# Windowed attention and gated feed-forward on one core: first loads of q and k in two pieces, a new load order, zero products in planned gaps, new priorities

## The chip, the cores and the metric

The kernel runs on one core of a Trainium2 chip. A core has TensorE (PE, matrix products, with a weight-load path shown as PEld), VectorE (DVE), ScalarE (ACT), GpSimd (POOL) and SyncE (SP), and 16 DMA engines that all queues share. POOL and SP issue the DMAs here. The metric is device time in microseconds (us), median over runs; the kernel before takes 314.26 us in the median of three runs (313.21 to 316.16).

## The reference

Eight batches of 576 tokens, eight heads of 64. Causal attention over a window of 64 tokens, and then a feed-forward layer with a ReLU gate over all 4608 tokens:

```python
scores = scale * np.matmul(q, k.transpose(0, 1, 3, 2))
mask = (rel >= 0) & (rel < window)          # rel = query - key, window = 64
attn = softmax(np.where(mask, scores, -1e9))
x = (attn @ v).transpose(0, 2, 1, 3).reshape(4608, 512)
gate = np.maximum(x @ w_gate, 0.0)          # w_gate, w_val: 512 x 1536
val = x @ w_val
out = (gate * val) @ w_out                  # w_out: 1536 x 512
```

## The kernel before

**Tiling.** The 4608 tokens are nine tiles of 512 (`TT`), counted 0 to 8. Attention goes by windows of 64 queries, nine to a batch (`NG`), eight to a tile; so tile 0 is windows 0 to 7 of batch 0, and tile 1 the last window of batch 0 and windows 0 to 6 of batch 1, which are its rows 0 to 447. A window's scores are products of transposed k and q (line 354, after a bias product that brings the mask, line 346); ACT takes the exponential into `p` (607); products of p with v and a column of ones give values and sums (360); DVE takes the reciprocal (622), normalises into `xw` (367) and transposes into `xt` (372).

**Feed-forward.** Tile 0 goes directly: products with `wg` and `wv` (712), ReLU on ACT (721), product of the two on DVE (723), output products (877). Tiles 1 to 8 use Strassen-like forms with seven products in place of eight (803 for gate and value, 965 for output from tile `TF` = 3 on). They need sums of weights `us`, `vs` (752), sums of x (678), and later `ts` (910). Results come out of PSUM by ACT copies (812, 850) and DVE sums (819); POOL multiplies gate and value (837).

**Loads.** q and k of a batch come as four loads, two names by two halves of the heads `hh`, 576 rows each: `qk_load` (316) on POOL, cast to 16 bits on the way, one partition holding 18 rows of one head. DVE transposes each with one instruction, `qk_trans` (322). v comes by `v_load` (325), the weights by `w_part` (306) in blocks of four column groups, two loads a block, and `wo_part` (309) in three blocks. In the first part q and k of `hh` = 0 go by SP without a cast into the space of `vs` (381), and ACT and DVE cast them (404).

**Order.** Nothing is left to a scheduler at run time. `first_part` (from line 376) is written by hand: tile 0's first six windows, with zero products (`PADS`, `keep_hot`) among them. Everything else is made by `second_part` as operations of a `Plan`: each has a due key, the engines that can do it with a duration for each, what it comes after, and what it takes and gives of pools (PSUM banks, buffers). `Plan.run` simulates the engines and issues, whenever an engine is free, the ready operation of the smallest key; that order becomes each engine's instruction stream. The engine then takes its stream in order, so an instruction that waits holds up all behind it on its engine. The keys are sums of constants in the table `K` (line 21), such as `T1` and `STEP` for when tile 1 and each later tile is due.

**What the plan knows of queues.** Loads on one queue follow one another in the plan (`dma=(MB, rate, queue)`); POOL has at most eight DMAs in flight. PE's instructions come in blocks of 256, which the plan fetches (`fetch`, `ASK`, `NEED`), counting two for each product of an operation's `count`. The runs of small products, scores and values, are put off if the fetch would be late. Before, the direct products of tile 0 (712) have no count.

Of the kernel before, what the change touches and what calls it, by code (L numbers as in the profile page):

```python
# [19 lines left out]

K = {"T1": 43.37, "STEP": 31.65, "wo1": 25.425, "wo2": 25.425, "q0": 0.14, "q1": 3.42, "q10": 0.5, "q11": -2.79, "v": 2.23, "v1": 24.04, "ql": 0.01, "qt": -1.77, "qti": 4.63, "vl": 1.83, "vc": 1.99, "vm": 1.89, "e": 6.47, "gap": 2.43, "gap1": -2.13, "r": -0.09, "tn": 2.56, "xf": 5.88, "wf": -6.38, "wfj": -2.26, "sn": 0.0, "su": -1.66, "re": 17.19, "mu": -7.51, "la": -4.87, "o0": 29.92, "o0j": 1.82, "o0s": -3.73, "oo": -0.002, "os": 0.141, "oj": 4.12, "gs": -2.63, "fo": -0.031, "fi": 0.104, "fs": 1.88, "fu": 1.51, "W0": 85.11, "TF": 3, "rs": -3.06, "rv": -0.95, "rt": -2.24, "slack": 0.3, "d2": 8.63}

# [4 lines left out]
class Op:  # L27


    def __init__(self, name, key, engines, fn, after, take, give, dma):  # L30
        self.small = 0
        self.count = 0
        self.name = name
        self.key, self.engines, self.fn = key, engines, fn
        self.take, self.give, self.dma = take, give, dma
        self.left = len(after)
        self.feeds = []
        self.ready = dict.fromkeys(engines, 0.0)
        self.end = None
        self.on = None  # L40


class Plan:
# [5 lines left out]
    TURN = 0.093  # L49
    FLIGHT = 8  # L50
# [4 lines left out]
    def __init__(self, free, queue, pools):  # L55
# [3 lines left out]
        self.home = {id(x[2]): name for name, items in self.pools.items() for x in items}  # L59
        self.known = {e: [] for e in free}  # L60
# [48 lines left out]

    def finish(self, o, e, t, dur):  # L110
        if e == "PE":
            dur += self.TURN * ((o.small > 0) != self.small)
            self.small = o.small > 0
            if o.count:
                dur = self.fetch(2 * o.count, t, dur, True) - t
# [25 lines left out]
    def grab(self, o, e, t):  # L141
# [7 lines left out]
        for holder, names, items in got:  # L149
            for name, item in zip(names, items):  # L150
                self.pools[self.home[id(item[2])]].remove(item)
                holder[name] = item[2]
        return None

    def pick(self, e, t):
# [6 lines left out]
        for o in sorted(self.known[e], key=lambda o: (o.key - self.STAY * (e == "PE" and self.small and o.small), o.n)):  # L162
            if o.ready[e] > t + 1e-9:
                continue
            if e == "POOL" and o.dma and self.flight[0] + 0.1 > t + 1e-9:
                continue
# [19 lines left out]
    def run(self, emit):  # L186
# [7 lines left out]
        while left:  # L194
# [3 lines left out]
            t = heapq.heappop(self.times)  # L198
            moved = True
            while moved:  # L200
                moved = False
                for e in ("PE", "ACT", "DVE", "POOL", "SP"):
# [9 lines left out]
                    if port:  # L212
                        other = "POOL" if e == "DVE" else "DVE"
                        begin = max(t, self.port[other])
                        self.port[e] = begin + dur
                    self.finish(o, e, begin, dur)
# [8 lines left out]
def kernel(  # L225
# [16 lines left out]
    G = 4  # L242
# [68 lines left out]
    def heads_of(b, name, hh):  # L311
        src = (q if name == "q" else k)[b, G * hh:G * hh + G]
        return src.rearrange("h (i j) d -> (h i) (j d)", i=32)

    def qk_load(b, name, hh):
        nc.gpsimd.dma_start(nat[name, hh], heads_of(b, name, hh))

    def qk_trans(b, name, hh):
        src = nat[name, hh].bitcast(FP32).rearrange("p (j e) -> p j e", e=32)
        dst = qTs[b % 2][:, hh] if name == "q" else kTs[b % 2][:, hh, 64:64 + S]  # L320
# [53 lines left out]
    PADS = 72  # L374

    def first_part():

        n = S // 32 * D
        t32 = {name: vs.rearrange("p a k n -> p (a k n)").bitcast(FP32)[:, n * i:n * i + n] for i, name in enumerate("kq")}
        for name in "kq":  # L380
            nc.sync.dma_start(t32[name], heads_of(0, name, 0))
        for name in "kq":
            qk_load(0, name, 1)
# [40 lines left out]
        qk_trans(0, "k", 0)  # L424
        rounded("q", nc.scalar.copy, nc.vector.tensor_copy)
        qk_trans(0, "q", 0)
        for name in "kq":
            qk_trans(0, name, 1)
# [18 lines left out]
        for hh in range(2):  # L447
            copies(0, nc.vector.tensor_copy, G * hh, G * hh + G)
            values(0, hh)
        copies(1, nc.gpsimd.tensor_copy, 0, H)  # L450
# [28 lines left out]
    def second_part():  # L479

        plan = Plan({"PE": 14.3, "ACT": 16.2, "DVE": 16.8, "POOL": 13.2, "SP": 3.0},
                    {"q": 16.4, "sp": 3.0},
                    {"bank": list(zip((13.4, 13.4, 15.2, 15.9, 12.9, 12.9, 12.9), banks)), "bo": [(14.2, banks[7])],
                     "p": [(13.8 if i < 8 else 0.0, p) for i, p in enumerate(ps)],
                     "pr": [(0.0, x) for x in prs]})
        plan.at = 428 + 2 * PADS
        plan.asked, plan.got, plan.come = 2, 1, [13.0, 22.2]
# [22 lines left out]

        T0 = 16.0
# [8 lines left out]
        for n, (wt, src, key) in enumerate(((wg, moe_w_gate, "g"), (wv, moe_w_val, "v"))):  # L520
            for blk in range(NF // 4):
                loaded[key, blk] = [None, None] if blk == 0 else [
                    op("w_load", 14.0 + 4.0 * blk + 2.0 * n + 0.1 * a, issue(0.7),
                       lambda e, wt=wt, src=src, blk=blk, a=a: w_part(wt, src, 4 * blk, 4 * blk + 4, a),
                       dma=(0.524, 0.40, "q")) for a in range(2)]
        for blk in range(NF // 4):
            loaded["o", blk] = [op("wo_load", (24.5, K["wo1"], K["wo2"])[blk], issue(0.75), lambda e, blk=blk: wo_part(4 * blk, 4 * blk + 4),
# [10 lines left out]
        def quad_key(t, hh):  # L538
            return period(t - 1) + (K["q0"], K["q1"])[hh] if t > 1 else T0 + K["q10"] + K["q11"] * hh

        def values_key(t):
            return period(t - 1) + K["v"] if t > 1 else T0 + K["v1"]

        def load_batch(b):
            need = quad_key(max(1, NG * b // 8), 0)
            for i, (name, hh) in enumerate((n, hh) for hh in range(2) for n in "kq"):
                before = [turns[b - 1, name, hh]] if b > 1 else []
                key = 24.6 + 0.1 * i if b == 1 else need - K["ql"] + i
                loads[b, name, hh] = op("qk_load", key, issue(0.57), lambda e, b=b, name=name, hh=hh: qk_load(b, name, hh),
                                        after=before, dma=(0.59, 0.40, "q"))  # L550
                turns[b, name, hh] = op("qk_turn", need - K["qt"] + K["qti"] * i, {"DVE": (1.245, False)},
                                        lambda e, b=b, name=name, hh=hh: qk_trans(b, name, hh),
                                        after=[loads[b, name, hh]] + (score_ops[b - 2] if b > 1 else []))

        def load_values(b):
            parts = {0: ((1, 0, 128), (3, 0, 128)), 1: ((5, 0, 128),), 2: ((7, 0, 128), (NG - 1, 64, 128))}
            for uu in range(UB):
                need = values_key(max(0, (NG * b + 3 * uu - 8)) // 8 + 1)
                if (b, uu) not in ((0, 0), (0, 1)):
                    for n, part in enumerate(parts[uu]):  # L560
                        key = {(0, 2): 16.9, (1, 0): 25.4, (1, 1): 25.41, (1, 2): 25.42 + 0.1 * n}.get((b, uu), need - K["vl"])
# [13 lines left out]
                elif b == 1:  # L575
                    vcopies[b, uu] = [op("v_copy", need - K["vc"], {"ACT": (0.17 + 0.42 * to.shape[1], False), "DVE": (0.1 + 0.2 * to.shape[1], True),
# [3 lines left out]
                else:  # L580
                    before = value_ops[b - 2] if b > 1 else []
                    vcopies[b, uu] = [op("v_move", need - K["vm"], {"SP": (0.6, False)}, lambda e, to=to, at=at: nc.sync.dma_start(to, at),
# [9 lines left out]
        def attend(items, key):  # L592
# [5 lines left out]
            after = [turns[b, nm, hh] for b in batches if b for hh in halves for nm in "kq"]  # L598
# [6 lines left out]
            for g in range(G):  # L605
                def exp(e, g=g):
                    nc.scalar.activation(pp[g][:, 0:n].rearrange("p n c -> p (n c)"), st[g][:, 0:64 * n], ACT.Exp, scale=scale)  # L607
                exps.append(op("exp", key + K["e"] + 0.6 * g, act(64 * n), exp, after=[run], take=[("p", pp, (g,))], give=[("bank", st, g)]))
            return pp, exps

        def value_bank(t, key, parts, before, gives, last):
# [19 lines left out]
            r = op("recip", key + K["r"], {"DVE": (0.17, False)}, recip, after=[a])  # L631
            return a, op("norm", key + K["r"] + 0.3, dve(64 * m), normed, after=[r] + last, give=[("bank", to, "b")])
# [4 lines left out]
        def attend_tile(t):  # L637
# [9 lines left out]
            gap = K["gap"] if t > 1 else K["gap1"]  # L647
# [16 lines left out]
            for hh in range(2):  # L664
                for i in range(2):
                    lo = 16 * hh + 8 * i
                    turned[t].append(op("turn", key + K["tn"] + gap * (1.2 * (2 * hh + i) + 1.7), {"DVE": (0.712, False)},
# [6 lines left out]
            for n, (x, y) in enumerate(((b12, b11), (b22, xc[:, 0]), (b22, b12), (b21, xc[:, 1]))):  # L674
                after = [(t11, t12), (t22,), (t22, t12), (t21,)][n] + tuple(free)
                after += tuple(forms[j] for j in {1: (0,), 3: (1,)}.get(n, ()))
                forms.append(op("x_form", key + K["xf"] * gap + n, {**pool(512), **(dve16(512) if n == 1 or t == 1 else {})},
# [3 lines left out]

        load_values(0)
        pp, masks = attend([(6 + i, hh) for hh in range(2) for i in range(2)], T0 + K["rs"])
        rest, before = [], []
        for hh in range(2):
            parts = [(24 + 4 * hh + s, pp, 6 + s // 2, hh, 2 * hh + s // 2, s % 2) for s in range(4)]
            gives = [("p", pp, g) for g in range(G)] if hh else []
            a, o = value_bank(0, T0 + K["rv"] + 0.3 * hh, parts, masks + before, gives, [])
# [378 lines left out]
```

## Time and profile before

The page describes one execution, which took 313.09 us; its span from first to last instruction is 311.1 us.

| what | us |
|---|---|
| median of three runs | 314.26 |
| the profiled execution, its span | 313.09, 311.1 |
| PE busy | 297.9 |
| DVE, POOL, ACT busy | 244.5, 228.0, 214.4 |
| POOL's product of gate and value, 96 times | 121.1 |
| score and value products, 1152 each, busy | 13.0 and 15.4 |
| transposes of q and k, 32 times, each | 1.24 |
| DMA issue on POOL for q or k, each | 0.57 to 0.58 |

Matmuls are pipelined: one of 256 columns shows 273 ns from start to modelled end, but in a row they start 109 ns apart. So busy time of PE tells where it has nothing to do at all, and not how dense it is. PEclk is the granted clock of TensorE. DMA share is the mean busy share of the 16 DMA engines, and can go over 1 where packets overlap. "issue" is time in which an engine waited for nothing that the profile shows. An entry "[1.05 <-DVE qT L322]" is idle time before an instruction and what ended it.

### The profile page before, as it was taken

The numbers are of one execution on the slowest core, as the hardware profiler recorded it, in microseconds if no ns is written. First come the engines' busy times: TensorE is split into PE (matmuls) and PEld (weight loads), VectorE is DVE, ScalarE is ACT, GpSimd is POOL, SyncE is SP. The second block draws the span as 40 slices with busy tenths as digits, with TensorE's granted clock in tenths as the row PEclk, the third lists the DMA queues.
The fourth block names the chain that finished last, engine by engine and source line by source line (L and its number), as shares of the span: only waits on it lengthen the run. The fifth ranks groups of instructions, "written<-read, shape, count | busy, mean of one in ns | idle before, by whom it ended". The sixth has DMA issues, their size and how long they took to land.

```text
span 311.1 us, 11209 instructions
## 1 busy us (share of the span) xinstructions
PE 297.9 (96%) x4749; PEld 240.4 (77%) x4749; DVE 244.5 (79%) x421; ACT 214.4 (69%) x415; POOL 228.0 (73%) x232
## 2 busy tenths in 40 slices
PE   7699969999999999999999999999999999999994
PEld 4487734588867786778888888888888888888883
DVE  5969986799946985887897999899876896674951
ACT  4553363598788589668868786888588968678731
POOL 8689896488997998699499946992479258737530
PEclk9889989999999999999999999999999999999999
DMA  7999998999139955777698183912102010121034
GB/s 216 188 174 206 194 198 144 197 201 101 28 31 192 188 117 112 124 120 104 94 108 100 52 152 62 138 52 68 39 2 71 15 59 2 36 67 36 1 103 135
DMA packets 58930, 32.87 MB, mean 106 GB/s; under 512 B 39424, under 2 KB 53248, under 8 KB 58880
## 3 DMA queue, kind: packets, MB, share of 16 engines
q0 software_dynamic: 46672, 18.29, 49.9%
q1 hardware_dynamic: 12208, 13.87, 14.2%
q8 instruction: 37, 0.61, 0.8%
q14 instruction: 13, 0.11, 0.1%
HBM read 37.75 MB, written 9.44 MB: 152 GB/s over the span
## 4 chain that ended last, share of the span: by engine, by line
PE 80%; DMA 10%; POOL 4%; DVE 2%; issue 2%; ACT 0%; SPq 0%; POOLq 0%; DVEq 0%; ACTq 0%
PE bank L803 46%; PE bank L965 18%; PE bank L877 9%; PE bank L360 4%; DMA q<-in_q_dram 3%; DMA wv<-in_moe_w_val_dram 2%; PE bank L354 2%; DMA v<-in_v_dram 2%; DMA v<-v 2%; PE bank L346 1%; POOL v L325 1%; DVE xt L372 1%; DVE xw L367 1%; POOL v L578 0%; POOL wg L306 0%
## 5 line engine op out<-in xcount | busy, mean ns | idle before, releaser
L837 POOL TENSOR_TENSOR g_sb<-pr,pr 128x512 f16<-128x512 f32 x96 | 121.1, 1278 | 48.7 <-ACT pr L850 18.1
L819 DVE TENSOR_TENSOR pr<-bank,pr 128x512 f32<-128x512 f32 x144 | 93.4, 682 | 33.5 <-PE bank L803 29.8
L812 ACT COPY pr<-bank 128x512 f32<-128x512 f32 x144 | 80.7, 589 | 35.6 <-PE bank L803 30.4
L803 PE MATMUL bank<-xt,us 128*128 128x256 f16 x384 | 56.2, 273 | 0.1
L803 PE MATMUL bank<-xt,vs 128*128 128x256 f16 x384 | 56.2, 273 | 0.0
L828 ACT ACTIVATE pr<-pr 128x512 f32<-128x512 f32 x72 | 45.0, 635 | 8.4 <-DVE pr L819 8.1
L803 PE MATMUL bank<-xt,wv 128*128 128x256 f16 x288 | 42.4, 272 | 0.1
L803 PE MATMUL bank<-xt,wg 128*128 128x256 f16 x288 | 41.9, 273 | 0.0
L803 PEld LDWEIGHTS <-us 128*128 128x128 f16 x384 | 37.1, 98 | 6.1 <-issue 0.3
L803 PEld LDWEIGHTS <-vs 128*128 128x128 f16 x384 | 37.0, 98 | 6.1
L607 ACT ACTIVATE p<-bank 128x512 f16<-128x512 f32 (+1 forms) x68 | 35.7, 591 | 7.0 <-PE bank L354 6.9
L877 PE MATMUL bank<-wo,g_sb 128*128 128x512 f16 x144 | 36.8, 393 | 0.0
L325 POOL DMA_DIRECT2D v<-in_v_dram x40 | 34.8, 877 | 0.3 <-DMA wo<-in_moe_w_out_dram 0.3
L850 ACT ACTIVATE pr<-bank 128x512 f32<-128x512 f32 x48 | 27.4, 596 | 6.8 <-PE bank L803 6.2
L803 PEld LDWEIGHTS <-wv 128*128 128x128 f16 x288 | 28.2, 98 | 4.1 <-issue 0.3
L803 PEld LDWEIGHTS <-wg 128*128 128x128 f16 x288 | 27.8, 98 | 4.0
L965 PEld LDWEIGHTS <-g_sb 128*128 128x128 f16 x288 | 27.5, 98 | 3.5
L965 PE MATMUL bank<-wo,g_sb 128*128 128x256 f16 x216 | 28.7, 273 | 0.0
L367 DVE TENSOR_TENSOR xw<-bank,r 128x448 f16<-128x448 f32 (+2 forms) x45 | 25.9, 576 | 1.5
L372 DVE STREAM_TRANSPOSE xt<-xw 128x512 f16<-128x512 f16 (+2 forms) x38 | 25.1, 671 | 0.5 <-ACT xw L473 0.3
L877 PEld LDWEIGHTS <-g_sb 128*128 128x128 f16 x144 | 13.9, 101 | 13.3 <-issue 2.2
L965 PEld LDWEIGHTS <-ss 128*128 128x128 f16 x216 | 21.1, 98 | 2.4
(95 smaller groups left out, 386.2 us busy)
## 6 DMA issues: line engine op xcount, KB each, us to landing
out_dram<-pr SPq DMA_DIRECT2D x35, 256.0 KB, 2.8
k<-in_k_dram POOLq DMA_DIRECT2D x15, 288.0 KB, 6.6
q<-in_q_dram POOLq DMA_DIRECT2D x15, 288.0 KB, 6.5
v<-in_v_dram POOLq DMA_DIRECT2D x32, 128.0 KB, 5.2
v<-v SPq DMA_DIRECT2D x12, 132.0 KB, 2.7
v<-v SPq DMA_DIRECT2D x24, 66.0 KB, 2.9
wg<-in_moe_w_gate_dram POOLq DMA_DIRECT2D x6, 256.0 KB, 6.8
wv<-in_moe_w_val_dram POOLq DMA_DIRECT2D x6, 256.0 KB, 8.4
```

Of the source, the lines that this page charges most:

```text
L325: nc.gpsimd.dma_start(v16s[b % 2][lo:hi, g, :, 0:64], v[b, :, 64 * g - 64 + lo:64 * g - 64 + hi].rearrange("h p d -> p h d"))
L367: nc.vector.tensor_tensor(x, blocks_of(to, n)[:, :, 0:D].rearrange("p s (c e) -> p s e c", e=2), r[:, :, :, None].to_broadcast([128, n, 2, ...
L372: nc.vector.transpose(xt[:, 2 * hh:2 * hh + 2, c0:c0 + n].rearrange("p e (s c) -> p s e c", c=32), x)
L607: nc.scalar.activation(pp[g][:, 0:n].rearrange("p n c -> p (n c)"), st[g][:, 0:64 * n], ACT.Exp, scale=scale)
L803: nc.tensor.matmul(slot[to][:, HT * m:HT * m + HT], w[:, kk, 128 * m:128 * m + 128], x[:, kk], start=(first and m == 0 and kk == 0), stop= ...
L812: lambda e, hold=hold, slot=slot: nc.scalar.copy(hold["x"], slot["A"]),
L819: nc.vector.tensor_tensor(hold["x"], slot[to], hold["x"], ADD)
L828: lambda e: nc.scalar.activation(hold["x"], hold["x"], ACT.Relu), after=[o])
L837: lambda e: VEC[e].tensor_tensor(gh[:, fs:fs + 2, h], pair(a["x"]), pair(b["x"]), MUL),
L850: lambda e, hold=hold, slot=slot, i=i: nc.scalar.activation(hold["x"], slot["A"], ACT.Copy if i else ACT.Relu),
L877: nc.tensor.matmul(bank["b"][:, 0:c1 - c0], gs[t % 2][:, f, 128 * sub:128 * sub + 128], wo[:, f, c0:c1], start=(j == 0 and i == 0), stop=( ...
L965: nc.tensor.matmul(bank[to][:, HD * m:HD * m + HD], a[:, f, 128 * m:128 * m + 128], b[:, f], start=(first and m == 0 and f == 0), stop=(f ...
```

## The change

What it does, in the order of the kernel:

1. **Pieces.** Loads and transposes of q and k take a start row and a count. Of batch 0, `first_part` loads, casts and transposes rows 0 to 383 alone; rows 384 to 575 are loaded and transposed by operations of the plan. Batch 1 comes as rows 0 to 447 and rows 448 to 575. Later batches come whole, as before. A score run comes after the pieces that its windows need.
2. **Load order.** Keys of the weights (`wl`, `wln`), of q, k and v of batches 0 and 1 (`l0` to `l3`, `lv`, `lvs`, `lv0`) and of `wo` (`wo0`, `wo1`, `wo2`) are constants of the table. In keys, batch 0's rest comes at 19.2, the weights at 17.7 to 23.4, the first block of wo at 22.9, batch 1's first pieces at 26.7 to 29.4 with v's first at 28.4, wo's second block at 33.5, batch 1's second pieces at 34.6, wo's third block at 136.8. POOL issues no DMA in the plan while its queue is more than `bl` = 9.0 us behind.
3. **Zero products.** Where the plan sees PE wait 0.7 us or more for the next operation, `fill` emits products of zeros of 384 columns, 0.165 us each in the plan, up to 0.25 us before it: into a bank that is free, or adding zero to an output bank that is open. `first_part` has one more `keep_hot`.
4. **Counts.** The direct products of tile 0 are counted for the fetch of instructions.
5. **Start of the plan.** All times at which the plan takes over are `FRONT` = 1.8 us earlier, and the arrivals of instruction blocks 10.3 and 17.0 in place of 13.0 and 22.2.
6. **Priorities.** All constants of `K` are new, and `kt` adds to most of them an offset for each tile (some 300 entries in `K["d"]`).

The diff, cut to its core:

```diff
+    def fill(self, o, t, emit):
+        if t - self.free["PE"] < 0.7:
+            return
+        free = [(self.taken[id(h[n])], h[n]) for pool, h, names in o.take if "bank" in pool for n in names]
+        free += [(x[0], x[2]) for pool in ("bank", "bo") for x in self.pools[pool]]
+        if free or self.open:
+            since, bank = min(free, key=lambda x: x[0]) if free else (0.0, self.open[-1]["b"])
+            since = max(self.free["PE"], since + 0.1)
+            n = int((t - 0.25 - since) / 0.165)
+            if n > 0:
+                self.fetch(2 * n, since, 0.165 * n, True)
+                emit((bank, bool(free)), n)
...
+            if e == "POOL" and o.dma and self.queue["q"] - t > K["bl"]:
+                heapq.heappush(self.times, self.queue["q"] - K["bl"] + 1e-3)
+                continue
...
+                    if e == "PE":
+                        self.fill(o, begin, emit)
...
-    def heads_of(b, name, hh):
-        src = (q if name == "q" else k)[b, G * hh:G * hh + G]
-        return src.rearrange("h (i j) d -> (h i) (j d)", i=32)
+    def heads_of(b, name, hh, t0, n):
+        src = (q if name == "q" else k)[b, G * hh:G * hh + G, t0:t0 + n]
+        return src.rearrange("h (i j) d -> h i (j d)", i=32)
+
+    def nat_of(name, hh, t0, n):
+        return nat[name, hh][:, t0 // 32 * D:(t0 + n) // 32 * D]
...
-            nc.sync.dma_start(t32[name], heads_of(0, name, 0))
+            nc.sync.dma_start(t32[name], heads_of(0, name, 0, 0, 2 * U))
         for name in "kq":
-            qk_load(0, name, 1)
+            qk_load(0, name, 1, 0, 2 * U)
...
+        keep_hot(banks[2][:, 0:2 * U])
         copies(1, nc.gpsimd.tensor_copy, 0, H)
...
-        plan.asked, plan.got, plan.come = 2, 1, [13.0, 22.2]
+        plan.asked, plan.got, plan.come = 2, 1, [12.1 - FRONT, 18.8 - FRONT]
...
+        def kt(name, t=None):
+            return K[name] + K["d"].get(f"{tile_now[0] if t is None else t}:{name}", 0.0)
...
+        PIECES = {0: ((2 * U, S - 2 * U),), 1: ((0, 448), (448, S - 448))}
...
+            for m, (t0, n) in enumerate(PIECES.get(b, ((0, S),))):
+                for i, (name, hh) in enumerate((x, hh) for hh in range(2) for x in "kq"):
+                    before = [o for _, o in turns[b - 1, name, hh]] if b else []
+                    key = {(0, 0): 16.0 + kt("l3"), (1, 0): 24.0 + kt("l0") + kt("l1") * (i // 2),
+                           (1, 1): 24.0 + kt("l2")}.get((b, m), need - kt("ql") + i) + 0.1 * i
...
+            ends = {b: 64 * max(w % NG for w, _ in items if w // NG == b) + 64 for b in batches}
+            after = [o for b in batches for hh in halves for nm in "kq" for t0, o in turns[b, nm, hh] if t0 < ends[b]]
...
+                ops[-1].count = NC * w
...
+            if not isinstance(o, Op):
+                for _ in range(e):
+                    nc.tensor.matmul(o[0][:, 0:384], zero[:, 0:128], zero[:, 0:384], start=o[1], stop=o[1], skip_group_check=True)
+                return
```

## Prediction

> **What bounds the kernel now.** I read the page first.
>
> ```profile
> PE 297.9 (96%) x4749; PEld 240.4 (77%) x4749; DVE 244.5 (79%) x421; ACT 214.4 (69%) x415; POOL 228.0 (73%) x232
> PE   7699969999999999999999999999999999999994
> PEclk9889989999999999999999999999999999999999
> ```
>
> TensorE is the bound, and after the first fifth it has no holes at this resolution. So the second view is busy time by stretches, cut where the digits dip (stretch, its length, busy time and count of each engine, granted clock, DMA share, GB/s).
>
> ```profile
> 13.97:17.39 3.42, 3.42 (x81) 2.70 (x66) 2.36 (x7) 1.78 (x7) 3.42 (x6) 0.50 1.63 182
> 17.39:39.24 21.85, 21.85 (x318) 16.69 (x316) 19.70 (x37) 8.99 (x21) 19.35 (x25) 1.00 1.32 193
> 39.24:44.40 5.16, 2.20 (x129) 1.59 (x128) 4.16 (x6) 4.75 (x9) 4.99 (x7) 1.00 1.49 199
> 44.69:48.11 3.42, 3.42 (x10) 1.20 (x9) 3.25 (x9) 0.00 (x0) 1.76 (x2) 0.50 1.33 209
> 58.30:61.50 3.20, 2.70 (x85) 2.00 (x85) 3.10 (x7) 2.33 (x5) 0.00 (x0) 1.00 1.31 221
> 61.50:295.20 233.70, 233.04 (x3652) 194.66 (x3651) 190.01 (x311) 182.08 (x341) 178.07 (x163) 1.00 0.50 83
> ```
>
> From 61.5 to 295.2 us PE is idle 0.66 us, 0.64 of it in one stretch from 100.0 to 102.2. A new order of the same products can gain nothing there; it can only lose. All that can be won lies before 61.5 us, and the third view, PE in order of time, shows where (start, length, idle before and releaser).
>
> ```profile
> 8.58 0.55 PE L354 MATMUL bank<-qT,kT 32*128 32x64 f16 x48 [0.55 <-DVE qT L322]
> 13.68 0.54 PE L360 MATMUL bank<-v,p 128*32 128x65 f16 x40 [1.08 <-POOL v L440]
> ...
> 41.23 0.61 PE L354 MATMUL bank<-qT,kT 32*128 32x64 f16 x56 [1.05 <-DVE qT L322]
> 41.78 0.25 PE L360 MATMUL bank<-v,p 128*32 128x65 f16 x8
> 42.41 0.21 PE L360 MATMUL bank<-v,p 128*32 128x65 f16 x2 [0.38 <-POOL v L578]
> 43.93 0.54 PE L360 MATMUL bank<-v,p 128*32 128x65 f16 x46 [1.32 <-issue]
> 44.41 6.18 PE L877 MATMUL bank<-wo,g_sb 128*128 128x512 f16 x20
> ```
>
> First scores at 8.58 wait for a transposed q; values at 13.68 for copies of v; then tile 1's attention stalls on the last transposed q of batch 1, on a copy of v, and on nothing that the profile shows. The chain of waits, in order of time, says what stands behind these.
>
> ```profile
> 5.86 6.36 DMA v<-in_v_dram
> ...
> 16.52 7.54 DMA wv<-in_moe_w_val_dram
> 24.60 10.69 DMA q<-in_q_dram
> 35.32 1.26 DVE qT L322
> ```
>
> Up to 44 us the chain runs through loads that queue behind one another. By the issues at line 316 and their times to landing, batch 1's k, q, k, q land at 33.9, 35.3, 36.7 and 38.1: one per 1.39 us at full flow.
>
> **What is lost, in rows.** At half clock from 13.97: 16 products of 192 columns take 2.2 us (15.45 to 17.7); the 16 from 19.11 step at 83 ns, 1.33 us: 0.85 lost. From 39.24: the score run took 2.5 us, the one from 58.96 on 0.75 to 0.84; 56 value products 2.6 against 0.57: 3.7 lost. At half clock from 44.69: 3.42/2 = 1.7. From 58.3: about 0.5. At 100: 0.64. Sum 7.4.
>
> **The change, part by part.** The sum is made against the profiled execution: 313.1 us, span 311.1, 2.0 around it; the median of three is 314.26, 1.2 above.
>
> *First part with 384 of 576 rows.* On DVE four transposes of 1.25 us stand nearly in a row from 5.61 to 10.7. At two thirds of the columns each is between 0.83 (proportional) and 0.90: line 372's transposes of 256, 384 and 512 columns take 0.45, 0.58, 0.71, so 0.19 of it is fixed, and 0.19 + 1.06 x 2/3 = 0.90. At 0.88, 4 x 0.37 = 1.5. The v loads land at 10.1, 11.0 and 12.2 behind four loads of q and k; a third of four times 1.39 is 1.85 less ahead of them, and POOL's copies and the loads queued behind them on POOL (line 325 at 13.58, weights at 15.12) move with them. The smaller decides: -1.5. Bounds: -1.85, and the third rival below for the loss.
>
> *The remaining 192 rows, and batch 1 as 448 + 128.* Eight more DMA issues on POOL at 0.57 (line 316) are 4.6 us; POOL is busy 19.35 of 21.85 us from 17.39, so about two fit and the rest delays later issues. These land some 10 us after issue behind a backlog, which hides that; without a backlog it costs up to 2.1. DVE gets four turns of 192 columns, 0.19 + 0.35 = 0.54 each, 2.2 us, and saves 4 x (1.25 - 1.01) = 1.0 on the pieces of 448: +1.2 in a stretch with 2.15 free. Batch 1's first pieces land 4 x 1.39 x 128/576 = 1.2 earlier, and v loads go between the two halves, so that values wait less. Zero by itself; it counts in the stall.
>
> *Stall from 39.24, 3.7 us.* Three causes, three edits: last qT 1.05 to 1.23 (pieces, earlier flow), v 0.38 to 0.6 (v earlier), 1.32 "issue" in the middle of a run of values. The last I read as instruction supply: the page's queue 8 has 37 packets for 0.61 MB, and 2 x 4749 PE instructions over 37 is 257 a packet; the plan counts these, but left out the 224 products of the direct blocks, which the change adds. What is late next is the rest of the queue: with PE 1.5 earlier, its direct products run into weights (wv block 1 lands at 24.1 and 24.8, its products start at 25.03), and scores need four banks while tile 0's output holds others. So not all: -2.4, bounds 0 and -3.7.
>
> *Zero products in gaps over 0.7 us, one more keep_hot.* The half clock after 44.69 follows a stretch in which PE was busy 2.20 of 5.16. A shorter stall, or one filled with products, should avoid it: -1.7, bounds 0 and -1.7. The same for 13.97, but keep_hot adds one product in a 1.08 us wait, where the last such (9.36) didn't keep that stretch at full clock: -0.4, bounds 0 and -0.85. The Trainium skill (TensorE: Matmul & The Clock Gate, Part 1) has free-running windows of about 3.4 us and a gate that closes after an idle one; the trace's two half stretches are 3.42 long, and by that rule this last term falls to 0 or 0.85 with the start of the run. The costs: a filler is 163 ns a product (384 columns, line 712), ends 0.25 before the planned next step, and holds back what is ready earlier than planned. No row shows one; the nearest is line 469's, 0.61 us between values and scores. Nil where the wait is real, three gaps by 0.5 where it isn't: +0.3, bounds 0 and 1.5.
>
> *Priorities by tile, wo1 and wo2 later.* Near 58.3 and 100 about 1.1 us is exposed: -0.6. In the dense stretch, eight tiles, whose order all changes: +0.2 if the new order is nearly as dense; up to eight stalls like 100's 0.64, 5.1, if not. wo's second and third block are moved back, but were issued behind batch 1's q and k already (34.66 and 35.59 on POOL), so nothing goes from ahead of these: 0. The third landed at 46.7; if it comes later, the banks that tile 0's output holds stay taken for as long. The tail from 307.0 to 311.1 (evacuations, stores) is untouched.
>
> Sum: -1.5 - 2.4 - 1.7 - 0.4 + 0.3 - 0.6 + 0.2 = -6.1. 313.1 - 6.1 = 307.0 for such an execution; on the median 314.26 - 6.1 = **308.2**.
>
> **Rivals.**
>
> *Everything fits* (0.14): all 7.4 plus 1.5 goes: 314.3 - 8.9 = 305.4, at 1.85 in front 305.0. For it: 61.5 to 295.2 shows that the plan can pack PE densely once data is there. Against: the flow to 44 us is full (193 to 199 GB/s), and the same bytes are needed but for 1.2 us.
>
> *Arrivals hide the front* (0.18): PE comes 1.5 earlier to weights and batch 1 that come no earlier, and the stall grows by what the front won. Left are 1.7 + 0.4 + 0.6 - 0.3 - 0.2 = 2.2: 312.1. For it: wv's landing on the chain at 24.06, and products that start right behind it. Against: q and k's third was ahead of those weights too.
>
> *Pieces that load slowly* (0.10, slower than before). A load of all 576 rows is one run of 128 equal rows, four heads without a hole; a piece leaves a hole after each head, so its outer count is 4. If a transfer is dealt out over the engines by that count, it has 4 of 16. Then a 384-row load takes 1.39 x 2/3 x 4 = 3.7 us, the two on SP 7.4 where they now take 2.8, and q lands at 6.24 + 4.6 = 10.8. Cast 0.3, transpose 0.88: scores at 12.0, 3.4 later than 8.58, and the front loses 3.3 where it should win 1.5. Batch 1's piece of 448 takes 4.3 in place of 1.1, so the stall stays. 314.3 + 3.3 - 1.7 - 0.4 - 0.6 + 0.5 = 315.4, and up to 317.5 if the clock isn't kept. It decides once the first scores come 2.2 us later than now, with q at about 8.9. Against: all loads of before are shaped for 128, so no row tells. The Trainium skill (DMA: Bandwidth & Descriptors, Rules for kernel authors, "Use all 16 engines") says that an outermost count below 16 confines a DMA to so many engines; no run here shows it yet.
>
> *The new order stalls in the dense stretch* (0.10): the plan's times are its own, and one wait a tile of 1.3 us, as with the "issue" above, is 10.4: 314.3 - 6.1 + 10.4 = 318.6. Against: 0.66 us of such waits in 233.7 now.
>
> **How the numbers follow.** Forecast 0.48, with its own range 305.5 to 311.5: the stall at its bounds makes it 306.9 to 310.6, half clocks and fillers about one more on either side. The range over all: 303.8 to 316.5. Its foot is the first rival's 305.0 less the 1.2 by which single executions stood below their median; its head takes in the third rival but its worst, and leaves out the fourth. One per cent, about what a measurement tells from no change, is 3.1 us: faster below 311.1, slower above 317.4. Faster: 0.14 and 0.48 and a part of the second rival, 0.06, less 0.01: 0.67. Slower: most of the fourth and the end of the third: 0.12. Same: 0.21.
>
> **What would show it.** Front: first direct product near 14.0 (15.45 now), transposes of 384 columns at 0.88, q's load on SP at 4 us or less; 7 or more is the third rival. Stall: score run of tile 1 in 0.84, no "issue" among values, batch 1's q down by 36.5. Clock: 1.00 through the 40s. Dense stretch: PE idle under 1 us over some 234 us; several are the fourth rival. I am wrong if PE idles as long as now before 61 us for new reasons, or if zero products stand where PE's next work was already ready.

## The result and the profile after

The changed kernel takes 323.8 us, median of four runs (323.05 to 324.47); beside it the kernel before took 315.21 (four runs, 313.21 to 316.56). The ratio is 1.0277, with a 95% interval of 1.0209 to 1.0345: slower by 8.6 us, where 308.2 was forecast. The profiled execution took 324.47 us (span 322.7), the highest of its four; that of before, 313.1, lies just below the lowest of its own. So the two spans differ by 11.6 us where the medians differ by 8.6. Medians are over all executions of a kernel; the ratios leave out the slow ones, more than 1.5% above its fastest (one of four in f1_b0pieces, of ten in e4_whole, of twelve in g4_hot).

The page of the changed kernel: busy time of the engines, PE in 40 slices, the granted clock, and the packets.

```profile
PE 300.3 (93%) x4764; PEld 241.6 (75%) x4764; DVE 249.6 (77%) x428; ACT 212.9 (66%) x414; POOL 236.4 (73%) x242
PE   5279998997999999999998999999999999999995
PEclk9999999999999999999999999999999999999999
DMA packets 65434, 32.69 MB, mean 101 GB/s; under 512 B 44904, under 2 KB 60520, under 8 KB 65384
```

PE has 2.4 us more work than before (297.9) but 9 us more idle time, and most of it stands in the first three slices: they are at 5, 2 and 7 where they were at 7, 6 and 9. The clock digits have no 8 left, so no half clock behind the front is the cause. Of the front they don't tell: the clock's record begins at 22.39 us in this trace (7.15 before), and where there is no record the page shows a 9.

PE in order of time, after, answers to the third view of before (start, length, idle before and releaser):

```profile
18.04 0.83 PE L388 MATMUL bank<-qT,kT 32*128 32x64 f16 x48 [6.49 <-DVE qT L356]
18.93 1.65 PE L456 MATMUL bank<-zero 128*128 128x384 f32 x2
...
22.49 0.91 PE L456 MATMUL bank<-zero 128*128 128x384 f32 x2
...
24.08 1.77 PE L762 MATMUL bank<-xt,wg 128*128 128x192 f16 x16
...
32.81 0.82 PE L1076 MATMUL bank<-zero 128*128 128x384 f16 x4
...
49.04 0.37 PE L380 MATMUL bank<-ident,biasT 32*128 32x256 f16 x5 [1.09 <-DVE g_sb L774]
...
55.07 0.31 PE L394 MATMUL bank<-v,p 128*32 128x65 f16 x16 [0.74 <-POOL v L626]
...
61.97 1.02 PE L928 MATMUL bank<-wo,g_sb 128*128 128x512 f16 x4 [0.41 <-DMA wo<-in_moe_w_out_dram]
```

The first direct product of before, for comparison:

```profile
15.45 2.41 PE L712 MATMUL bank<-xt,wg 128*128 128x192 f16 x16
```

The first scores come at 18.04 (8.58 before), the first direct product at 24.08 (15.45): 8.63 us are lost in front, the size of the whole result. Behind the first direct product the two executions differ by 3.0 us more, 298.6 against 295.7. The waits there are other ones than before, all short. Two equal zero products take 1.65 us at 18.93 and 0.91 at 22.49, so from 18 to 22.4 PE ran at about half the speed that it had behind it.

The chain of waits, after, in order of time (start, length, what), shows what stands behind both:

```profile
1.62 14.94 DMA vs<-in_q_dram
...
38.88 11.10 DMA k<-in_k_dram
...
56.25 5.67 DMA wo<-in_moe_w_out_dram
...
73.25 7.14 DMA v<-v
...
161.80 7.95 DMA out_dram<-pr
```

It now begins with q's first load on SP, 384 rows for one half of the heads. It lands at 16.56; the whole 576 rows landed at 6.24 before, by the issues of before (KB each, us to landing):

```profile
vs<-in_q_dram SPq DMA_DIRECT2D x1, 576.0 KB, 5.0
```

Fewer bytes take three times as long. POOL's loads are late too; after:

```profile
k<-in_k_dram POOLq DMA_DIRECT2D x2, 224.0 KB, 12.0
...
k<-in_k_dram POOLq DMA_DIRECT2D x1, 192.0 KB, 14.0
```

The 192 KB are batch 0's; whole, its k and q took 6.5 and 7.2 in that place. The 224 KB are batch 1's, and its whole loads took 10.4 to 11.2 before, behind a backlog, so that this row shows little. Batch 0's v lands at 17.3 to 18.9 (10.1 to 12.2 before), the last q of batch 1's first pieces at 50.3 (38.1).

By stretches (length; busy time and count of PE, PEld, DVE, ACT, POOL; clock; DMA share; GB/s), after, up to its first direct product and behind it:

```profile
0.00:24.08 24.08, 12.49 (x287) 7.50 (x288) 9.38 (x26) 6.63 (x22) 13.42 (x27) 1.00 0.86 121
24.08:50.00 25.92, 24.37 (x372) 18.63 (x371) 19.74 (x45) 9.55 (x25) 21.32 (x26) 1.00 1.63 172
50.00:100.00 50.00, 47.03 (x764) 32.81 (x763) 43.69 (x74) 33.34 (x63) 46.08 (x50) 1.00 1.01 141
100.00:200.00 100.00, 97.79 (x1629) 78.10 (x1627) 85.54 (x134) 76.31 (x144) 82.33 (x82) 1.00 0.73 110
```

and before, up to its own:

```profile
0.00:15.45 15.45, 10.48 (x325) 6.86 (x326) 11.54 (x30) 7.71 (x26) 11.22 (x24) 0.95 1.21 202
```

The front moves 121 GB/s where it moved 202.

### The profile page after: what moved, and what is told of

Its sections match the earlier page's. It is cut to its first block, busy times and chain, and to the rows that moved or that the text cites. A ratio compares the mean times of both kernels' runs of the same rounds, so it can differ in the third digit from the quotient of the medians.

```text
span 322.7 us, 11251 instructions
## 1 busy us (share of the span) xinstructions
PE 300.3 (93%) x4764; PEld 241.6 (75%) x4764; DVE 249.6 (77%) x428; ACT 212.9 (66%) x414; POOL 236.4 (73%) x242
## 4 chain that ended last, share of the span: by engine, by line
PE 78%; DMA 15%; ACT 2%; POOL 2%; DVE 1%; issue 1%; SPq 0%; ACTq 0%
PE bank L854 43%; PE bank L1017 16%; PE bank L928 7%; DMA vs<-in_q_dram 5%; PE bank L394 4%; DMA k<-in_k_dram 3%; PE bank L762 3%; DMA out_dram<-pr 2%; PE bank L388 2%; DMA v<-v 2%; DMA wo<-in_moe_w_out_dram 2%; PE bank L380 1%; POOL vs L803 1%; PE bank L456 1%; DVE qT L356 1%
## 5 line engine op out<-in xcount | busy, mean ns | idle before, releaser
L888 POOL TENSOR_TENSOR g_sb<-pr,pr 128x512 f16<-128x512 f32 x96 | 120.5, 1275 | 47.7 <-DVE pr L870 12.2
L854 PE MATMUL bank<-xt,vs 128*128 128x256 f16 x384 | 55.4, 273 | 1.7 <-ACT pr L863 1.7
L854 PE MATMUL bank<-xt,us 128*128 128x256 f16 x384 | 55.5, 273 | 0.4 <-issue 0.4
L656 ACT ACTIVATE p<-bank 128x512 f16<-128x512 f32 (+1 forms) x68 | 36.5, 592 | 11.1 <-PE bank L388 11.0
L928 PE MATMUL bank<-wo,g_sb 128*128 128x512 f16 x144 | 35.9, 379 | 0.4 <-DMA wo<-in_moe_w_out_dram 0.4
L1017 PEld LDWEIGHTS <-g_sb 128*128 128x128 f16 x288 | 27.9, 98 | 3.3
L356 DVE STREAM_TRANSPOSE kT<-k 128x576 f32<-128x576 f32 (+4 forms) x20 | 20.3, 1015 | 3.9 <-DMA k<-in_k_dram 3.8
```

What stands on the lines that cost most here:

```text
L854: nc.tensor.matmul(slot[to][:, HT * m:HT * m + HT], w[:, kk, 128 * m:128 * m + 128], x[:, kk], start=(first and m == 0 and kk == 0), stop= ...
L888: lambda e: VEC[e].tensor_tensor(gh[:, fs:fs + 2, h], pair(a["x"]), pair(b["x"]), MUL),
L928: nc.tensor.matmul(bank["b"][:, 0:c1 - c0], gs[t % 2][:, f, 128 * sub:128 * sub + 128], wo[:, f, c0:c1], start=(j == 0 and i == 0), stop=( ...
L1017: nc.tensor.matmul(bank[to][:, HD * m:HD * m + HD], a[:, f, 128 * m:128 * m + 128], b[:, f], start=(first and m == 0 and f == 0), stop=(f ...
```

## The experiments

Two theories at the start. **A**: the piece loads run on few transfer engines (the third rival), and all of the loss is in front. The other, that the loss comes from the new order of the plan, is called C in the first expectations and D from f1_b0pieces on; B there is that a piece is slow for another reason than the count of engines. Each ratio is to the kernel before on the same chip, with its interval.

**e1_heads.** Each head of batch 0's first pieces loaded by itself, so that no load has a hole.

```diff
-            nc.sync.dma_start(t32[name], heads_of(0, name, 0, 0, 2 * U))
+            for g in range(G):
+                nc.sync.dma_start(t32[name][32 * g:32 * g + 32], heads_of(0, name, 0, 0, 2 * U)[g])
```

The same on POOL for the other half.

> The changed kernel, with each of the first part's four loads of 384 rows issued as four loads of one head each (32 equal rows, no hole), so that its outer count is 32 in place of 4; the plan and its order stay. Theory A (a load with an outer count of 4 runs on 4 of 16 engines; k and q on SP and k on POOL share the same four, 96 packets of 0.134 us = 12.9 us): q on SP lands at 6 to 7.5 us (16.6 now), first direct product at 14.5 to 16.5 (24.1 now), and the time falls by 8 us or more, to 316 or below. Theory B (a piece is slow because it is a smaller transfer, or more of them): q lands at 15 or later, and the time stays at 323 or above. Theory C (the new order is what costs): the front gets faster, but the span behind the first direct product stays at some 298 us or grows.

322.11 us, 1.0192 [1.0119, 1.0265]. PE in order of time:

```profile
7.26 0.41 PE L447 MATMUL bank<-ident,bias 128*32 128x128 f16 x8 [3.91 <-DVE bias L437]
...
16.82 1.77 PE L764 MATMUL bank<-xt,wg 128*128 128x192 f16 x16
...
19.78 1.33 PE L764 MATMUL bank<-xt,wv 128*128 128x192 f16 x14 [0.94 <-DMA wv<-in_moe_w_val_dram]
```

q lands at 7.87 in place of 16.56, with packets of the same 3072 bytes, and the first direct product comes 7.26 earlier, so A's mechanism holds for the front. PE's 4764 products stand in the order of the changed kernel. But the end gains only 1.7 by the medians (2.7 by the ratios, whose intervals overlap), where A expected 8: POOL's eight issues hold back the bias (3.91 idle before 7.26) and the loads behind them, and PE runs into weights, then into waits of 1.19 and 1.10 us for `g_sb` up to 45.85 and a half clock behind them. Here a front that was won alone was mostly given back at the next arrivals.

**e2_pairs.** SP's loads cut into two heads each, `heads_of(...)[g:g + 2]` for g = 0 and 2: an outer count of two.

> The changed kernel, with the two SP loads of the first part issued as two loads of two heads each (outer count 2). Theory A: two engines carry all of k and q, 128 packets each and 32 of POOL's k beside them, 160 x 0.134 = 21 us: q lands at 20 to 25 us (16.6 now), and the time rises by 5 us or more, to 329 or above. Theory B: q lands as now or later by under 1 us, the time within 2 us of 324.

333.53 us (one run). The chain begins:

```profile
2.71 22.24 DMA vs<-in_q_dram
```

q lands at 24.95: 6.24 with 128 equal rows, 16.56 with four groups, 24.95 with two. The same bytes, dealt out in two groups, come later than in four: the outer count decides. The packet records of the traces agree: in nearly every moment SP's queue has at most 4 packets in flight in the changed kernel and at most 2 here; before it had 16 at a time and more.

**e3_b0whole.** Batch 0 whole again, and the plan's start and instruction arrivals as before; batch 1 still in pieces, everything else as changed.

```diff
-            nc.sync.dma_start(t32[name], heads_of(0, name, 0, 0, 2 * U))
+            nc.sync.dma_start(t32[name], heads_of(0, name, 0, 0, S))
...
-    FRONT = 1.8
+    FRONT = 0.0
```

> The changed kernel, with batch 0 loaded whole in the first part as before (576 rows, outer count 128), no rest to load, and the plan's start and instruction arrivals as before; batch 1 still in pieces of 448 and 128 rows, new keys, counts and zero products kept. Theory A: q on SP lands at 6.2, first direct product at 15.4, time 8 us or more below 324; batch 1's q still takes 2 to 3 us longer to land than whole. Theory C: 298 us or more behind the first direct product, time 314 or above.

331.13 us, 1.0491 [1.0416, 1.0566]. q lands at 6.53 and the first direct product comes at 16.37, 7.7 earlier than after, and yet the kernel is 7.3 slower than after. It has long waits that nothing in the trace releases:

```profile
55.31 0.36 PE L394 MATMUL bank<-v,p 128*32 128x65 f16 x12 [3.34 <-issue]
...
76.67 0.20 PE L388 MATMUL bank<-qT,kT 32*128 32x64 f16 x2 [0.85 <-issue]
```

and half clocks from 53.95 to 60.8. The planner had made another order from the same keys. The run can't price batch 0's pieces; that it can't is its lesson, and the cleaner runs below take the keys of before.

**e4_whole.** As e3_b0whole, with `PIECES = {}`: no pieces at all, but new keys, counts and zero products.

> As the run before it, and batch 1 whole too: no pieces at all, new keys, counts and zero products kept. Theory A: as fast as the run with batch 1 in pieces or faster by 1 to 3 us. Theory C: 298 us or more behind the first direct product, time 314 or above; if instead the new order is worth what was forecast for it beside the front (4.6 us), the time is 308 to 311.

319.36 us, 1.0111 [1.0072, 1.015]. The first direct product comes at 16.86; the rest of the change without pieces doesn't win. It stalls for 1.80 us ahead of 66.94, for a copy of v, and for 1.10 ahead of 163.17, with half clocks from 12.98 to 19.8 and 67.6 to 74.4.

**f1_b0pieces.** The other side: keys, counts and order of before, no zero products, and only batch 0 in pieces.

```diff
+        PIECES = {0: ((2 * U, S - 2 * U),)}
...
-            nc.sync.dma_start(t32[name], heads_of(0, name, 0))
+            nc.sync.dma_start(t32[name], heads_of(0, name, 0, 0, 2 * U))
```

> The kernel before (its keys, no zero products in gaps, no counts), with batch 0 alone in pieces as in the change: 384 rows in the first part, 192 in the plan, outer count 4. Theory A (the four-engine loads are the whole cost): q on SP lands at 16 to 17 us, first direct product at 23 to 25, and the median is 6 to 9 us above before, 321 to 324. Theory D (the late front is mostly made up for behind it, since loads of batch 1 hold PE at 39 us anyway, and the new order is the cost): the median is under 3 us above before, 318 or less.

323.87 us, 1.0258 [1.0175, 1.0341]: the changed kernel's time. Of PE's 4749 products 148 stand at another place than before, all between the 285th and the 650th.

```profile
18.14 0.83 PE L388 MATMUL bank<-qT,kT 32*128 32x64 f16 x48 [6.31 <-DVE qT L356]
...
24.18 1.77 PE L761 MATMUL bank<-xt,wg 128*128 128x192 f16 x16 [0.42 <-DVE xt L406]
```

The front is the changed kernel's within 0.1 us, and 8.7 behind before's. This is the cleanest run: batch 0's pieces alone make the whole loss, and the rest of the change nets about nothing on top of them, as far as two ratios with intervals of 0.7 to 0.8% on either side can tell (some 3 us).

**f2_oldkeys.** The changed kernel with the old values of `K` and `d` empty.

> The changed kernel (pieces of both batches, zero products, counts) with the keys of before and no offsets by tile. Theory A: within 2 us of the changed kernel, 322 to 326. Theory D: faster than it by 3 us or more, 320 or less.

335.25 us, 1.064 [1.0571, 1.071]. Neither theory had this. The front is late as well (scores at 18.20, first direct product at 25.46); the planner emits 66 zero products in place of 13, 12.4 us of PE by the profile (2.6 for the 13). Old keys don't fit a plan with late pieces.

**f3_fillcount.** Before, plus `fill` and the counts; the last `keep_hot` is not in it.

> The kernel before with zero products in gaps and counts of the direct products alone; whole loads and old keys. If these two do what was forecast, the granted clock is 1.00 from 40 to 50 us, the 1.3 us wait in tile 1's values goes, and the median is 2 to 4 us below before, 311 to 313. If the gap moves elsewhere, 314 to 317.

322.74 us, 1.0228 [1.0147, 1.0309]: the expected gain didn't come. The front is before's (15.47), only two zero products are emitted, but counting the direct products shifts the fetches, the plan is made anew, and new waits appear:

```profile
24.96 4.44 PE L761 MATMUL bank<-xt,wg 128*128 128x384 f16 x16 [2.01 <-DVE xw L401]
...
52.14 0.30 PE L394 MATMUL bank<-v,p 128*32 128x65 f16 x16 [1.38 <-DVE g_sb L773]
```

**f4_nofill.** The changed kernel without the call of `fill`.

> The changed kernel without the zero products in gaps (13 products, 2.1 us of PE). If they stand in real waits and keep the clock, it is 0 to 3 us slower than the changed kernel, 324 to 327, with a half clock of 3.4 us somewhere before 90 us; if they hold PE's next work back, it is 1 to 2 us faster, 322 to 323.

339.75 us, 1.0784 [1.0719, 1.0849]. Missed too. Thirteen zero products alone don't make 16 us: of PE's 4672 other products 2420 stand at another place, and PE is idle for 11.2 us between 25 and 100 us (4.4 in the changed kernel) and 7.2 between 100 and 200 (2.2). From f2, f3 and f4 follows only that the keys don't carry over to another plan than their own; what each part is worth by itself they can't say.

**g1_spfour and g2_poolfour.** Before's keys; only SP's half of batch 0 (g1) or only POOL's (g2) in pieces. The idea was that the two halves' loads of four groups take the same four engines, so that one half alone would be fast.

> The kernel before, with batch 0's first half of the heads alone in pieces (k and q on SP, outer count 4, 192 rows later on POOL); the other half whole on POOL. If POOL's k shares SP's four engines in the changed kernel, it is missing here: 64 packets of 0.134 us from 2.0 us on, q lands at 10 to 12 us (16.6 with both), first direct product at 17 to 20 us, median 2 to 5 us above before. If SP's loads are slow by themselves, q lands at 16 or later and the median is 8 us or more above.

> The kernel before, with batch 0's second half of the heads alone in pieces (k and q on POOL, outer count 4, cast on the way); k and q on SP whole. With 32 packets on each of four engines for k and as many on others for q: POOL's k and q land at 8 to 11 us, first direct product at 15.4 to 17.5, median 0 to 2.5 us above before. The two halves alone then cost less in sum than the 9 us of both together. If POOL's pieces are the ones that hold the queue behind them, the median is 5 us or more above.

g1: 322.01 us, 1.0257 [1.0229, 1.0286]; its chain begins

```profile
1.62 15.49 DMA vs<-in_q_dram
```

so that q lands at 17.1 though POOL's k and q are whole: the idea falls. g2: 316.51 us, 1.0102 [1.0057, 1.0148]; SP's q lands at 6.38, POOL's k and q at 10.47 and 10.78 (7.8 and 9.2 before), and

```profile
12.06 0.55 PE L388 MATMUL bank<-qT,kT 32*128 32x64 f16 x48 [1.26 <-DVE qT L356]
...
15.79 2.86 PE L764 MATMUL bank<-xt,wg 128*128 128x192 f16 x16
```

The front loses 0.34 there, as POOL's half is wanted later. The 1.0% of g2 lies behind the front, where a half clock of 6.83 us begins at 13.22 (3.42 us before). SP's two loads alone (g1) cost what all four did (f1), so nearly all of the loss comes with them. That goes for POOL's late v as well: batch 0's v loads take 12.8 to 12.9 us in the changed kernel and 13.4 to 13.5 in g1, where POOL's own k and q are whole, but 6.9 to 7.1 in g2, where only POOL's are in pieces.

**g3_mix.** The changed kernel with SP's loads by head (as e1_heads) and POOL's half of batch 0 whole, `qk_load(0, name, 1, 0, S)`.

> The changed kernel, its order unchanged, with the first part's loads off the four engines: k and q on SP one head a load, on POOL 576 rows whole (the rest of 192 rows is loaded again as planned). q on SP lands at 7 to 8.5 us, first direct product at 15.5 to 17. If the front is what the change loses and its order then fits, the median is 6 us or more below the changed kernel, 317.5 or less. If arrivals of weights and batch 1 hold the order back as with one head a load on both queues (322.1), it is 320 or more.

318.82 us, 1.0149 [1.0094, 1.0204]. q lands at about 9.4, the first direct product comes at 17.92, 6.2 earlier than after, and 4 to 5 us of it reach the end (1.0149 against 1.0277; by the medians 5.0): between the two cases that were expected. PE's 4764 products stand in the order of the changed kernel. The best of the changed order, and still behind before: 2.5 of 4.7 us are in front, and it waits 1.88 us at 46.5 for a copy of v.

**g4_hot.** Before's order, with eight zero products of 384 columns ahead of tile 1's second run of scores and eight ahead of its first run of values: does work in the stall alone keep the clock?

```diff
+                for _ in range(8):
+                    nc.tensor.matmul(bank[:, 0:384], zero[:, 0:128], zero[:, 0:384], start=True, stop=True, skip_group_check=True)
```

> The kernel before in its own order, with eight zero products of 384 columns ahead of tile 1's second score run and eight ahead of its first value run (2.6 us of PE in the stall of 39.2 to 44.4 us). If filling a wait keeps the clock, it is 1.00 from 44.7 to 48.1 and the median is 0.8 to 1.7 us below before (ratio 0.995 to 0.9975). If the zeros hold real products back or shift the supply of instructions, the ratio is 0.999 to 1.006.

315.15 us, 1.0029 [0.9997, 1.006]: no gain. The stall and what follows it, by stretches:

```profile
39.24:43.77 4.53, 2.61 (x82) 1.54 (x80) 4.49 (x7) 3.95 (x9) 4.40 (x6) 1.00 1.55 195
43.77:47.19 3.42, 3.24 (x63) 1.62 (x63) 0.21 (x1) 0.52 (x2) 2.94 (x4) 0.50 1.35 205
```

PE is busy for 2.61 of 4.53 us there (2.20 of 5.16 before), the 1.3 us "issue" wait stays, and the half clock comes for the same 3.42 us. But the stall was filled in part only: of the eight zero products ahead of the values two ran before that wait (at 42.10) and six behind it, from 43.95 on and so at half clock. Whether a filled stall keeps the clock is not shown.

**h1_alone.** What stayed open was the size: the rival had 3.7 us a load, and the pair took 15. g1's kernel, with POOL's loads held back until SP's q has landed.

```diff
-        for name in "kq":
-            qk_load(0, name, 1, 0, S)
...
         bands()
+        nc.gpsimd.tensor_copy(nat["k", 1][:, 0:1], t32["q"][:, 0:1])
+        for name in "kq":
+            qk_load(0, name, 1, 0, S)
```

> The kernel is g1_spfour's (keys of before, SP's k and q of batch 0 as 384 rows with a hole after each head, the rest as loads of their own), and POOL issues none of its loads until SP's q has landed: a copy on POOL of one column of q stands ahead of them. So two loads of 128 packets of 3072 B are alone in the transfer engines. In g1_spfour these took until 17.1 us beside POOL's loads, 64 packets in 15 us on each of four engines, 0.235 us a packet, where a packet itself took 0.12 to 0.134 us. Theory A (four engines, each shared half and half with POOL's queue): alone the packets follow one another at their own length, 32 x 0.134 = 4.3 us for k and as much for q, and with the first packet at about 2 us q lands at 10.5 to 11.5 us. Theory B (a load of four parts is slow by itself, whatever runs beside it): q lands at 16 us or later as before. The whole kernel is slower than g1_spfour in A, by how much later POOL's half of q and k, v and the weights come: they start about 11 us in place of 4, the first scores of the second half come after 16 us; 325 to 340 us under both.

323.79 us (one run). The chain begins

```profile
1.62 10.14 DMA vs<-in_q_dram
```

and the stretch in which SP's loads run alone:

```profile
3.00:11.00 8.00, 4.79 (x31) 2.13 (x29) 1.21 (x2) 0.84 (x3) 0.00 (x0) 1.00 0.25 96
```

96 GB/s at a DMA share of 0.25: four of sixteen engines, all the time, and by the packet records 4 packets in flight. (Before's SP loads ran at 338 GB/s and a share of 0.98 from 2.0 to 5.5 us.) q lands at 11.76, 5.3 earlier than in g1, by A within 0.3. The pair's packets run from 2.3 to 11.2 us, so a load on four engines takes about 4.4 us alone; the 5.3 more in g1 come with POOL's loads beside it, and the changed kernel's q, at 16.56, is late by nearly as much. The whole kernel doesn't gain, since POOL's own loads now start 11 us later.

## Why the prediction was wrong

**The step that failed is the first term**, "First part with 384 of 576 rows", -1.5. It measured +8.6 (the first direct product at 24.08 in place of 15.45). It took the time of a load to go with its bytes, from 1.39 us for the 576 rows. What decides instead is the outer count of the access pattern: a piece leaves a hole after each head, so it is four groups and runs on four engines. The mechanism stood among the rivals ("Pieces that load slowly"), with its place and its sign, at a chance of 0.10. The text argued from the pattern, and set against it only that no row of before shows such a load; an absent row is no evidence against, and the chance was too low for that. It had named 7 us or more for q's load on SP as its sign; that load took 14.94. The other half of the term, the transposes, held: with 384 columns they took 0.82 to 0.85 us where 0.88 was reckoned.

The Trainium skill's rule that the prediction cited beside it (DMA: Bandwidth & Descriptors, Rules for kernel authors, "Use all 16 engines") agrees with the runs: an outer count of four gave q at 16.56 and a DMA share of 0.25 when alone, a count of two 24.95.

**The rival's size was off as well**: q at 10.8, 315.4 in the end. Alone, it is 11.8 (h1_alone), so the price of the four engines was right to 1 us. Missing was that POOL's queue runs on the same engines at the same time: 16.6 to 17.1. Of the front's 8.6 us the rival priced 3.3. The Trainium skill (DMA: Bandwidth & Descriptors, Queues, rings and completion order) says that an engine takes packets of its queues in turn; g1_spfour against h1_alone agrees with it, 15.49 us beside POOL's loads and 10.14 without.

**The remaining rows and batch 1**, priced at zero: batch 1's last q landed at 50.3, 12.2 later than before, where the forecast wanted it by 36.5. Its own pieces are not what made it late: it took 9.5 us from issue to landing, 11.2 before, but was issued at 40.75, 13.9 later. In f1_b0pieces, where batch 1 is whole and the order nearly before's, the last q lands at 48.1, so 10 of the 12.2 us come with batch 0's pieces alone.

**The stall, -2.4.** It left its place: tile 1's scores run in 0.74 at 49.16, inside the 0.84 that was asked, and no "issue" stands among its values. But waits of 0.32 and 1.09 us up to 49.04 and of 0.74 ahead of 55.07 are in its stead. Between 25 and 100 us PE is idle for 4.38 us, 3.48 before. What was late next was named (weights, the rest of the queue); in fact it was `g_sb`, copies of v and wo.

**The clock, -1.7 and -0.4.** The first was right: 1.00 from 22.4 us to the tail, and no half clock behind tile 1's attention. Which edit did it is open: g4_hot put products into before's stall, filled it in part, and the half window came nevertheless. The second was not won: from 18 to 22.4 us PE ran at about half speed (two zero products in 1.65 us, 0.91 behind it), where before had 1.00 from 7.15 to 13.97. Full speed came late in all runs with SP's loads on four engines or fewer, its record beginning at 22.4 to 31.8 us.

**Zero products, +0.3.** Thirteen were emitted, by the plan's 0.165 us each 2.1 us of PE; whether each stood in a real wait can't be told from f4_nofill, whose plan is another.

**Priorities, -0.6 and +0.2.** Too hopeful: from 100 to 200 us PE is idle for 2.2 us, 0.64 before. The largest wait, 1.68 ahead of 170.48, ends a chain through a store of 7.95 us. So the fourth rival came true in a small part; what the late front adds to it was not separated.

Together: -1.5 became +8.6, and all other terms, forecast at -4.6, came to about zero, as f1_b0pieces (the pieces of batch 0 alone, 1.0258) against the changed kernel (1.0277) shows, or to a small loss: in the profiled executions the part behind the first direct product grew by 3.0 us.

## What to carry to other kernels

Before a load is cut into pieces, write down the outer count of what is left: a hole between groups can turn 128 equal rows into four groups, and such a load took four engines here and shared them with POOL's queue. Price a load beside what runs at the same time, not by its bytes alone. In a kernel whose order is made by a planner from tuned keys, a part that is switched off makes another plan; only versions that leave the order as it was or nearly so (here e1 and g3, f1, g1 and g2) can price a part.

## What was not expected of the hardware

- q's 384 KB on four engines, behind k's, landed 10.1 us after its issue when the two were alone and 14.9 to 15.5 beside POOL's queue. POOL's v loads beside them took 12.8 to 13.5 us, 6.0 to 7.1 where SP's loads were whole.
- A clock of one half came for 3.42 us after a stretch in which PE was busy for 58% (g4_hot, 2.61 of 4.53).
- Waits of up to 3.34 us ahead of small products that no event in the trace releases (e3_b0whole, before 55.31); that they are waits for instructions was argued, not isolated.
